# Reordering the head and the tail of a fused attention and gated-MLP kernel

## The chip, the cores and the metric

The kernel runs on one core of one Trainium2 chip. The metric is the device time in microseconds (us): the median over the runs of one kernel. Each profile shows one run, and its span is about 1.8 us shorter than the device time of that run (before: 782.7 us and 784.45 us). PE is the matmul engine (TensorE), PEld its weight load, DVE is VectorE, ACT is ScalarE, POOL is GpSimd, SP is SyncE; a q after the name means the instruction queue of that engine.

## The reference

All tensors are bf16. S is 2048, D is 512, there are 32 heads of width 16 with one shared key and value head, and F is 1792.

```python
def _A_ref(x, wq, wk, wv, wo):
    q = (x @ wq).reshape(B, S, H, Dh).transpose(0, 2, 1, 3)
    k = x @ wk
    v = x @ wv
    scores = jnp.einsum("bhqd,bkd->bhqk", q, k) * (Dh ** -0.5)
    o = jnp.einsum("bhqk,bkd->bhqd", _softmax(scores, axis=-1), v)
    return o.transpose(0, 2, 1, 3).reshape(B, S, H * Dh) @ wo

def _B_ref(x, w_gate, w_up, w_down):
    return (_silu(x @ w_gate) * (x @ w_up)) @ w_down

xn = _layernorm(x)
s = _A_ref(xn, A_wq, A_wk, A_wv, A_wo)
g = _silu(_B_ref(xn, B_w_gate, B_w_up, B_w_down))
return x + s * g
```

## The kernel before

A planner in the kernel orders all instructions when the program is built. It uses assumed durations and arrival times. `ext(t)` is an assumed arrival time, `chain` and `tadd` pin an instruction behind the one before it on the same engine. The body is a stream of 128x1024 exponentials on ACT. PE fills gaps with matmuls whose weights `zw` are zero, which is meant to keep its clock full.

The parts that the change and the argument touch (cuts are marked with `# ...`):

```python
PB_URG, AHEAD, LAZY, ACTMIN, ACTLOW = 6, 16, 8, 1.7, 1.5
# ... head: masks, loads
nc.vector.tensor_single_scalar(out=hbit[:], in_=pidx[:], scalar=DH, op=ALU.bitwise_and)
# ... two more DVE operations make hmask from hbit
nc.sync.dma_start(out=x_sb[:, 0:2, :], in_=x_v[:, 0:2, :])
nc.sync.dma_start(out=x_sb[:, 2:4, :], in_=x_v[:, 2:4, :])
# ... key, query and value weights on ACT's queue; the rest of x on SyncE
# ... blocks 2 and 3 of x: block 3's mean and variance are worked out on ACT
arr2 = ext(4.6)
a = OP("ACT", 0.65, [arr2], lambda: nc.scalar.activation(
    out=hT[:, 3, :], in_=x_sb[:, 3, :], func=ACT.Copy, accum_out=ssum[:, 0:1]), (-1,), name="asum")
# ... then a Square with accumulation; then DVE's veps of blocks 2 and 3 waits for both
# ... the planner's rule for zero matmuls: fill a gap when PE's recent activity is low
if Tz - F >= MMF + sd.switch("c") and act_ < ACTMIN:
    ...  # return F, ("zero", bb)
# ... tail
tadd("PE", tq_emit(1, [0, 1], tq01))          # transposes of the last block, f32
tadd("PE", tq_emit(1, [2, 3], tq23))
tadd("PE", e_out_mm(LN + 3, bank[st["obank"][3]][:, :D], range(NQ - 1)))   # 12 partial matmuls
# ... normalise, transpose o_tok, copy, final 8 matmuls, flag matmul
def fin_add(k, eng, nm):
    tadd(nm, e_out_add(LN + k, dsts[k], eng))
    bi = (nc.sync if k % 2 == 0 else nc.scalar).dma_start(out=out_v[:, LN + k, :], in_=res[(LN + k) % 4][:, :D])
    tadd("SP" if k % 2 == 0 else "ACT", bi)
# ... additions 0 and 2 on POOL, 1 and 3 on DVE, flag_i written between
flag = nc.values_load(flag_i[0:1, 0:1], min_val=0, max_val=1)
with tc.If(flag > 0):
    ...  # exact-maximum fallback, never taken with these inputs
```

## Time and profile before

Before the change: 785.91 us median of 3 runs (785.13 to 789.57). The profiled run had 784.45 us.

| part of the span, us | before |
|---|---|
| first statistics on x start | 3.64 |
| first statistics to first exponential | 9.83 |
| first exponential to end of the last (the body) | 755.43 |
| end of last exponential to end of DVE's last addition | 9.15 |
| from there to the end of the span (the closing) | 4.65 |
| of the body at half clock | 6.8 |

The five parts add up to the span, so a difference between two profiles can be put in one of them. The prediction below shows the lines. The timeline of the kernel before: its columns are start, duration, engine, source line, operation, tiles, and in brackets the idle time before it and what ended it.

### The profile page before, as it was taken

How to read it: one execution, taken by the hardware profiler on the slowest of the kernel's cores; microseconds unless marked ns; L12 is line 12 of the kernel's file. 1: busy time of each engine (PE TensorE's matmuls, PEld its weight loads, DVE VectorE, ACT ScalarE, POOL GpSimd, SP SyncE). 2: the span in 40 equal slices, each digit the busy share in tenths (PEclk: the TensorE clock that was granted, in tenths of full speed). 3: DMA queues.
4: the chain of work that ended last, by engine and by line, in shares of the span. 5: the costliest groups of instructions: out<-in, count | busy, mean ns of one | idle time of the engine just before them, and what ended most of it. 6: DMA issues, size and time to landing. Idle time of an engine off the chain costs nothing.

```text
span 782.7 us, 19544 instructions
## 1 busy us (share of the span) xinstructions
PE 699.4 (89%) x8149; PEld 209.0 (27%) x8150; DVE 732.4 (94%) x920; ACT 758.0 (97%) x866; POOL 50.6 (6%) x59
## 2 busy tenths in 40 slices
PE   7988888899898898999899898899988989899994
PEld 3322222222222222222222222222222222222221
DVE  7779999999999999999999999999999999999994
ACT  5999999999999999999999999999999999999993
POOL 3100000000011000000002000000001200000001
PEclk9999999999999999999999999999999999999997
DMA  9400000000011000000001000000000000000000
GB/s 328 138 9 9 15 2 23 2 10 15 3 43 35 23 1 8 18 1 16 10 23 36 22 23 2 23 3 9 17 1 23 30 22 2 1 23 2 23 2 31
DMA packets 21191, 20.07 MB, mean 26 GB/s; under 512 B 8744, under 2 KB 17192, under 8 KB 21096
## 3 DMA queue, kind: packets, MB, share of 16 engines
q1 hardware_dynamic: 19224, 17.94, 7.5%
q8 instruction: 65, 1.06, 0.6%
q10 hardware_dynamic: 1872, 0.82, 0.4%
q14 instruction: 30, 0.25, 0.1%
HBM read 14.19 MB, written 2.34 MB: 21 GB/s over the span
## 4 chain that ended last, share of the span: by engine, by line
ACT 52%; PE 26%; issue 12%; DVE 8%; DMA 1%; SPq 0%; POOL 0%; ACTq 0%; DVEq 0%
ACT Pb L934 46%; PE m_ps L485 10%; PE ring L874 10%; PE o_ps L744 5%; ACT th L654 4%; DVE Bf L988 2%; ACT th L671 1%; DVE x_sb L1007 1%; DVE Bf L1007 1%; ACT g_sb L934 1%; DMA x_sb<-in_A_x_dram 1%; DVE Bf L1014 0%; DVE Bf L1002 0%; DVE x_sb L988 0%; DVE ab L656 0%
## 5 line engine op out<-in xcount | busy, mean ns | idle before, releaser
L934 ACT ACTIVATE Pb<-ring 128x1024 bf16<-128x1024 f32 x772 | 726.0, 1133 | 3.7 <-PE ring L874 3.5
L874 PE MATMUL ring<-QB,KT 32*128 32x512 bf16 x2048 | 306.3, 384 | 60.3 <-ACT Pb L934 57.6
L988 DVE TENSOR_SCALAR Bf<-ring 128x1024 uint16<-128x1024 f32 x172 | 209.6, 1219 | 11.0 <-PE ring L874 9.2
L874 PEld LDWEIGHTS <-KT 32*128 32x128 bf16 x2048 | 92.8, 91 | 350.9 <-issue 346.9
L744 PE MATMUL o_ps<-Pb,VA 128*32 128x512 bf16 x1544 | 148.1, 385 | 0.7 <-ACT Pb L934 0.7
L1007 DVE TENSOR_TENSOR Bf<-Bf,Bf 128x2048 f16<-128x2048 f16 x74 | 90.0, 1216 | 0.1
L988 DVE TENSOR_SCALAR x_sb<-ring 128x1024 uint16<-128x1024 f32 x72 | 87.7, 1218 | 2.4 <-PE ring L874 2.2
L485 PE MATMUL m_ps<-xnT,wu_sb 128*32 128x512 bf16 x896 | 72.6, 387 | 5.2 <-DVE ab L656 5.2
L485 PE MATMUL m_ps<-wd_sb,hT 128*32 128x512 bf16 x896 | 71.5, 383 | 1.2 <-DVE g_sb L673 1.2
L485 PE MATMUL m_ps<-xnT,wg_sb 128*32 128x512 bf16 x896 | 71.5, 384 | 0.0
L744 PE MATMUL o_ps<-Bf,VD 128*32 128x512 f16 x688 | 67.9, 387 | 0.9 <-DVE Bf L1014 0.6
L729 POOL TENSOR_TENSOR oT<-oa,rb 128x512 bf16<-128x512 f32 x15 | 20.1, 1342 | 615.1 <-DMA rb<-dscr 410.5
L1014 DVE TENSOR_SCALAR Bf<-Bf 128x2048 uint16<-128x2048 uint16 x86 | 59.0, 686 | 0.5
L744 PEld LDWEIGHTS <-VA 128*32 128x32 bf16 x1560 | 38.3, 94 | 51.7 <-issue 50.1
L1002 DVE TENSOR_SCALAR Bf<-Bf 128x2048 uint16<-128x2048 uint16 x74 | 50.5, 687 | 0.0
L660 DVE TENSOR_TENSOR hT<-ab,m_ps 128x512 bf16<-128x512 f32 x56 | 38.1, 680 | 3.2 <-PE m_ps L485 3.1
L656 DVE SCALAR_TENSOR_TENSOR ab<-th,m_ps 128x512 f32<-128x512 f32 x56 | 38.1, 680 | 3.1 <-ACT th L654 3.0
L654 ACT ACTIVATE th<-m_ps 128x512 f32<-128x512 f32 x56 | 39.6, 706 | 0.0
L744 PEld LDWEIGHTS <-VD 128*32 128x32 f16 x976 | 26.2, 94 | 41.0 <-issue 37.7
L1007 DVE TENSOR_TENSOR x_sb<-x_sb 128x2048 f16<-128x2048 f16 x24 | 30.8, 1284 | 0.0
L744 PE MATMUL o_ps<-x_sb,VD 128*32 128x512 f16 x288 | 28.0, 386 | 1.1 <-DVE x_sb L1007 0.9
L485 PEld LDWEIGHTS <-wu_sb 128*32 128x32 bf16 x896 | 19.0, 95 | 34.2 <-issue 30.4
(115 smaller groups left out, 381.8 us busy)
## 6 DMA issues: line engine op xcount, KB each, us to landing
rb<-dscr SPq DMA_DIRECT2D x15, 256.0 KB
dn<-oa SPq DMA_DIRECT2D x120, 2.0 KB, 1.7
oa<-oa SPq DMA_DIRECT2D x60, 32.0 KB, 2.0
wg_sb<-in_B_w_gate_dram SPq DMA_DIRECT2D x1, 1792.0 KB, 12.5
wu_sb<-in_B_w_up_dram SPq DMA_DIRECT2D x1, 1792.0 KB
wd_sb<-in_B_w_down_dram SPq DMA_DIRECT2D x1, 1792.0 KB, 19.4
out_dram<-xn SPq DMA_DIRECT2D x14, 128.0 KB, 1.7
x_sb<-in_A_x_dram SPq DMA_DIRECT2D x3, 512.0 KB
```

The lines of the kernel that those rows point to most:

```text
L485: return [nc.tensor.matmul(out=dst[GRP * j:GRP * j + GRP, :], lhsT=w[:, GRP * j:GRP * j + GRP], rhs=rhs, start=start, stop=stop, tile_posi ...
L654: t_ = OP("ACT", 0.477, [a], lambda: nc.scalar.activation(out=th[i][:], in_=m_ps[:], func=ACT.Tanh, scale=0.5), (0,), name="tanh")
L656: s_ = OP("DVE", 0.6, [t_, ab_rel[i]], lambda: nc.vector.scalar_tensor_tensor(out=ab[i][:], in0=th[i][:], scalar=1.0, in1=m_ps[:], op0=ALU ...
L660: h = OP("DVE", 0.6, [b], lambda: nc.vector.tensor_tensor(out=hT[:, f, :], in0=ab[i][:], in1=m_ps[:], op=ALU.mult), (1,), name="hmul")
L729: return [pk, q], lambda eng: eng.tensor_tensor(out=oT[qs % 2][:, jj, :], in0=o0[:], in1=rbt[:], op=ALU.mult)
L744: r.append(nc.tensor.matmul(out=o_ps[GRP * g:GRP * g + GRP, :], lhsT=lhs, rhs=rhs, start=(n == 0), stop=(n == pv_total[(b, g)] - 1), tile_ ...
L874: return lambda: [nc.tensor.matmul(out=ring[sl][:, u * 512:(u + 1) * 512], lhsT=KT[half][GRP * g:GRP * g + GRP, t * P:(t + 1) * P], rhs=QB ...
L934: lambda: nc.scalar.activation(out=buf, in_=ring[i][:], func=ACT.Exp, scale=escale, bias=ebias),
L988: lambda: nc.vector.tensor_scalar(out=U[:, hs], in0=ring[si][:], scalar1=ubias, scalar2=UINF, op0=ALU.add, op1=ALU.min), (1.5, u), name="p ...
L1002: o1 = OP("DVE", 0.6, [pa, pa0] + wrel, lambda: nc.vector.tensor_scalar(out=Bf[wi], in0=U, scalar1=0x3FF, scalar2=0x3800, op0=ALU.bitwise_and,
L1007: return lambda: eng.tensor_tensor(out=Bf[wi][:, a:z].bitcast(FP16), in0=Bf[wi][:, a:z].bitcast(FP16), in1=U[:, a:z].bitcast(FP16), op=ALU ...
L1014: o2 = OP("DVE", 0.6, o3, lambda: nc.vector.tensor_scalar(out=U, in0=U, scalar1=0x7C00, scalar2=None, op0=ALU.bitwise_and), (2, u, 1), nam ...
```

## The change

The intent: shorten the head by loading the first rows of x ahead of the query weights and making the masks early; keep PE's clock full in the tail by issuing the partial product ahead of the transposes and adding filler matmuls; and issue all last stores from SyncE. Before the change, too, the first load of x was issued (0.72 us) ahead of that of the query weights (1.32 us). The diff, cut to its core:

```diff
-    nc.vector.tensor_single_scalar(out=hbit[:], in_=pidx[:], scalar=DH, op=ALU.bitwise_and)
+    mask_i = [None] * 3
+    mask_i[0] = nc.vector.tensor_single_scalar(out=hbit[:], in_=pidx[:], scalar=DH, op=ALU.bitwise_and)
 # ... mask_i[1], mask_i[2] likewise; the loads on ACT's queue get chain("ACT", ...),
 # ... with the warm-up activation between the key weights and the query weights
+    chain("DVE", mask_i)
-                arr2 = ext(4.6)
+                arr2 = ext(4.9)
-        if Tz - F >= MMF + sd.switch("c") and act_ < ACTMIN:
+        if Tz - F >= MMF + sd.switch("c") and (act_ < ACTMIN or cur["issued"] == NTILE):
+    tadd("PE", e_out_mm(LN + 3, bank[st["obank"][3]][:, :D], range(NQ - 1)))
     tadd("PE", tq_emit(1, [0, 1], tq01))
     tadd("PE", tq_emit(1, [2, 3], tq23))
-    tadd("PE", e_out_mm(LN + 3, bank[st["obank"][3]][:, :D], range(NQ - 1)))
+    for _ in range(2):
+        tadd("PE", nc.tensor.matmul(out=tp[0], lhsT=ident_bf[:], rhs=xnT[:, 0, 0:512], start=True, stop=True))
 # ... in fin_add
-        bi = (nc.sync if k % 2 == 0 else nc.scalar).dma_start(out=out_v[:, LN + k, :], in_=res[(LN + k) % 4][:, :D])
-        tadd("SP" if k % 2 == 0 else "ACT", bi)
+        tadd("SP", e_out_st(LN + k))
     fin_add(0, nc.gpsimd, "POOL")
     tadd("DVE", e_out_mul(LN + 1, obk[1], dsts[1]))
+    fin_add(1, nc.gpsimd, "POOL")
     tadd("DVE", e_out_mul(LN + 2, obk[2], dsts[2]))
-    fin_add(2, nc.gpsimd, "POOL")
     tadd("DVE", nc.vector.tensor_single_scalar(out=flag_i[:], in_=tq01[0:1, 0:1], scalar=P - 0.5, op=ALU.is_lt))
-    fin_add(1, nc.vector, "DVE")
     tadd("DVE", e_out_mul(LN + 3, obk[3], dsts[3]))
+    fin_add(2, nc.vector, "DVE")
     fin_add(3, nc.vector, "DVE")
```

More of the change, by code (lines that the diff above doesn't have):

```diff
@@ L323 @@
     warm = const.tile([P, 1], FP32, name="warm")
-    nc.scalar.activation(out=warm[:], in_=eps_t[:], func=ACT.Exp)
+    warm_i = nc.scalar.activation(out=warm[:], in_=eps_t[:], func=ACT.Exp)
     neg_half = const.tile([P, 8], FP32, name="neg_half")
@@ L330 @@
     hbit = const.tile([P, 1], I32, name="hbit")
-    nc.vector.tensor_single_scalar(out=hbit[:], in_=pidx[:], scalar=DH, op=ALU.bitwise_and)
+    mask_i = [None] * 3
+    mask_i[0] = nc.vector.tensor_single_scalar(out=hbit[:], in_=pidx[:], scalar=DH, op=ALU.bitwise_and)
     hmask = const.tile([P, 2], FP32, name="hmask")
-    nc.vector.tensor_scalar(out=hmask[:, 1:2], in0=hbit[:], scalar1=1.0 / DH, scalar2=None, op0=ALU.mult)
-    nc.vector.tensor_scalar(out=hmask[:, 0:1], in0=hbit[:], scalar1=-1.0 / DH, scalar2=1.0,
-                            op0=ALU.mult, op1=ALU.add)
+    mask_i[1] = nc.vector.tensor_scalar(out=hmask[:, 1:2], in0=hbit[:], scalar1=1.0 / DH, scalar2=None, op0=ALU.mult)
+    mask_i[2] = nc.vector.tensor_scalar(out=hmask[:, 0:1], in0=hbit[:], scalar1=-1.0 / DH, scalar2=1.0,
+                                        op0=ALU.mult, op1=ALU.add)
     xnT = persist.tile([P, KC, S], BF16, name="xnT")
@@ L407 @@
     with nc.allow_non_contiguous_dma(reason="tiny k/v weight loads (32B rows)"):
-        nc.scalar.dma_start(out=wk_sb[:], in_=A_wk.rearrange("(kc p) n -> p kc n", p=P))
-        nc.scalar.dma_start(out=wq_sb[:], in_=A_wq.rearrange("(kc p) n -> p kc n", p=P))
-        nc.scalar.dma_start(out=wv_sb[:], in_=A_wv.rearrange("(kc p) n -> p kc n", p=P))
+        chain("ACT", nc.scalar.dma_start(out=wk_sb[:], in_=A_wk.rearrange("(kc p) n -> p kc n", p=P)))
+        chain("ACT", warm_i)
+        chain("ACT", nc.scalar.dma_start(out=wq_sb[:], in_=A_wq.rearrange("(kc p) n -> p kc n", p=P)))
+        chain("ACT", nc.scalar.dma_start(out=wv_sb[:], in_=A_wv.rearrange("(kc p) n -> p kc n", p=P)))
     for c in range(1, NSC):
```

## The prediction

> **What bounds the kernel now.** I read the page first, then the busy time by stretches, then the timeline of the first 24 us and of the last 28 us, and last the chain of work that ended last and the branch instructions at the end. The page's busy line says which engine paces the body:
>
> ```profile
> PE 699.4 (89%) x8149; PEld 209.0 (27%) x8150; DVE 732.4 (94%) x920; ACT 758.0 (97%) x866; POOL 50.6 (6%) x59
> ```
>
> ACT is busy 97% of the span, nearly all of it in the 128x1024 exponentials (772 of them, 1133 ns each, overlapping, one every 0.90 us). Between the first exponential at 13.47 us and the last, which ends at 768.90 us, the kernel runs at ACT's pace, and the change touches nothing there. So only three things can move the time: the 13.47 us before the first exponential, the 13.8 us after the last (782.7 - 768.9), and accidents in the body. The stretches show the accidents:
>
> ```profile
> core 0: us, PE busy (x) PEld busy (x) DVE busy (x) ACT busy (x) POOL busy (x), PEclk, DMA share, GB/s
> 120.00:130.00 10.00, 8.79 (x92) 2.23 (x88) 8.78 (x11) 9.00 (x11) 0.00 (x0) 0.83 0.09 18
> ...
> 750.00:760.00 10.00, 9.69 (x98) 2.69 (x93) 9.04 (x14) 9.13 (x11) 0.00 (x0) 0.85 0.00 0
> ...
> 771.00:773.00 2.00, 1.82 (x16) 0.43 (x8) 1.76 (x10) 0.30 (x2) 0.00 (x0) 0.50 0.00 0
> ```
>
> The granted clock falls to half for 3.4 us twice in the body, and each time ACT loses about 1 us (9.00 and 9.13 busy of 10). A third drop lies in the tail, from 770.1 to 773.4 us: there PE runs at 0.50 for the whole stretch from 771 to 773. The head looks like this:
>
> ```profile
> 5.64 0.73 POOL L441 TENSOR_TENSOR rstd<-veps,neg_half 128x2 f32<-128x2 f32 x1 [0.29 <-DVE veps L438]
> ...
> 7.09 0.17 DVE L438 TENSOR_SCALAR veps<-mv 128x2 f32<-128x2 f32 x1 [0.73 <-ACT hT L530]
> ...
> 7.48 0.73 DVE L444 TENSOR_SCALAR xn<-x_sb,mv,rstd 128x512 bf16<-128x512 bf16 x2
> ...
> 8.70 0.59 ACT L455 COPY xnT<-ring 128x512 bf16<-128x512 bf16 x1 [1.55 <-PE ring L449]
> ...
> 13.47 7.44 ACT L934 ACTIVATE Pb<-ring 128x1024 bf16<-128x1024 f32 x8 [0.48 <-PE ring L874]
> ```
>
> DVE normalises the first two blocks of x (the xn line) at 7.48 us. Their scale factor (POOL's rstd) was ready at 5.64 + 0.73 = 6.37 us. The 1.1 us between is queue order: ahead of xn stands the veps of blocks 2 and 3, which waits for ACT's variance until 7.09 us, and then three mask operations that could have run in DVE's 2.4 us of idleness before x arrives at 3.64 us. The first copy of xnT and the first exponential hang on that xn. The tail:
>
> ```profile
> 769.86 1.02 PE L1042 MATMUL ring<-ident_f,oa 128*128 128x128 f32 x4 [0.52 <-DVE oa L757]
> ...
> 770.81 1.47 PE L485 MATMUL ring<-wo_sb,oT 128*32 128x512 bf16 x12
> ...
> 772.21 0.39 PE L1326 MATMUL ring<-ident_bf,o_tok 128*128 128x128 bf16 x2
> ...
> 773.94 1.29 DVE L687 SCALAR_TENSOR_TENSOR ab<-ring,g_sb 128x512 f32<-128x512 f32 x2 [0.87 <-PE ring L485]
> ...
> 775.91 1.59 POOL L692 TENSOR_TENSOR xn<-oa,x_sb 128x512 bf16<-128x512 f32 x1
> ...
> 777.12 0.93 DVE L692 TENSOR_TENSOR xn<-oa,x_sb 128x512 bf16<-128x512 f32 x1
> ```
>
> After the last block's transposes (L1042) PE runs 12 matmuls of a partial product (L485) at half clock until 772.28 us; only then come the transposes of o_tok (L1326), although their first half was written at 771.71 us. The final products end at 773.88 us, DVE multiplies from 773.94 us and ends the last addition at 778.05 us. What follows is no longer computing:
>
> ```profile
> L1359 SPq TENSOR_LOAD <-flag_i x1: 511/511/511, 776.4 to 776.4; - x1
> ...
> L1359 ACTq TENSOR_LOAD <-flag_i x1: 477/477/477, 778.5 to 778.5; - x1
> ```
> ```profile
> L1360 SPq COMPARE_BRANCH  x1: 45/45/45, 777.9 to 777.9; - x1
> L1360 ACTq COMPARE_BRANCH  x1: 54/54/54, 779.0 to 779.0; - x1
> ...
> L1360 ACTq EVENT_SEMAPHORE  x1: 17/17/17, 781.6 to 781.6; - x1
> ```
>
> ACT issues the last store at 778.08 us, loads the flag (0.48 us), compares at 779.0 us and is next seen at 781.6 us: 2.6 us for a jump. SyncE jumps at 777.9 us and is back at 780.7 us. The span ends about 1.0 us after ACT is back.
>
> **What the Trainium skill says.** "TensorE: Matmul & The Clock Gate", Part 1, has the clock fall to half after an idle window of about 3.4 us, a window that is free-running and not tied to the kernel's start. The trace agrees: 770.1 to 773.4 us is 3.3 us, and the drop near 125.0 us lies about 189 windows of 3.413 us earlier. "GPSIMD Engine Reference", 1 Specifications, has POOL share SBUF interfaces with DVE when a DVE instruction has two SBUF inputs; the trace agrees, as POOL's addition takes 1.15 us alone and 1.59 us beside DVE's additions. "Runtime: NRT & Kernel Launch", Instruction fetch mechanics, says that a taken branch outside the fetched pages stalls for a fetch; 2.6 and 2.8 us here fit it. "DMA: Bandwidth & Descriptors", Latency and other measured facts, gives a register load a floor of about 600 ns; here it took 0.48 to 0.67 us, so the measured numbers are used.
>
> **The change, part by part.** I compared the instruction order of both kernels on every engine.
>
> *Head.* On ACT nothing moves: before the change, too, the table load and the warm-up stand between the key-weight load and the query-weight load, and the x loads are untouched on SyncE. Worth 0. On DVE the masks move into the idle time, and the first two xn come ahead of the second veps, since the planner now assumes a later arrival (4.9 instead of 4.6). On POOL the building of ident_f (0.35 us) moves ahead of rstd: it starts about 5.40 us, so rstd runs from about 5.77 to 6.50 us. Then xn goes at 6.54 us instead of 7.48 us, its second one ends at 7.27 us, PE's eight transposes end at about 7.72 us and ACT copies at 7.76 us instead of 8.70 us: 0.94 us earlier. ACT is free then, its variance work ends at 7.16 us. The second scale factor, ready about 8.2 us, comes before DVE's copy ends at about 8.8 us, so it does not bind. One query-weight matmul (0.11 us apart at this size) now stands ahead of the next transposes and gives back about 0.13 us. First exponential: 13.47 - 0.94 + 0.13 = 12.66 us, a gain of 0.8 us. The query weights landed 5.8 us after issue at 1.32 us, so at about 7.1 us, before their new use at 9.3 us. The gain passes through the body whole, as no transfer is waited for there: the gate weights land 12.5 us after 3.80 us and are first used at 46.5 us.
>
> *Tail, PE.* Twenty zero matmuls (five groups of four) stand before the last accumulation. A group takes about 0.22 us at full clock: 5 x 0.22 = 1.1 us from 767.65 us, done by 768.75 us, before the last exponential releases the accumulation at 768.95 us. Cost 0. The 12 partial matmuls (3 groups, 0.65 us) now fill 769.17 to 769.82 us, while DVE copies the accumulator; the transposes start at 769.86 us as before. PE is now busy enough that I expect the clock to stay full. Then: transposes end at 770.67 instead of 770.88 us (gain 0.2); o_tok's halves are written at 771.49 and 772.13 us; its first transposes end at about 771.88 instead of 772.60 us; ACT copies at 771.92 instead of 772.70 us; the final eight matmuls start at 772.33 instead of 773.12 us and take 0.60 instead of 0.76 us. DVE's multiplications start at about 772.98 instead of 773.94 us: gain 0.95 us.
>
> *Tail, DVE, POOL, SyncE.* DVE has the same four multiplications, flag and two additions, with one wait less, and ends at about 776.95 instead of 778.05 us. That would be 1.1 us. But the queue behind it changes. POOL has additions 0 and 1 back to back: 773.82 to 774.97, then to between 776.1 us (alone) and 776.5 us (slowed by DVE's additions). SyncE, in order, issues store 1 after that (0.35), loads the flag (0.51, with some 0.1 for two small instructions), issues stores 2 and 3 (0.35 each) and compares: 1.75 us with gaps, so at 776.3 + 1.75 = 778.05 us. It is back 2.8 us later at 780.85 us, checks eight DMA semaphores in 0.6 us (as from 780.7 to 781.3 us before), and the closing barrier takes 0.9 us: 782.35 us against 782.7 us. Of the 1.1 us won on DVE only 0.35 us reaches the end.
>
> Sum: 0.8 + 0.35 = 1.15 us.
>
> **Rivals.** (a) *The stores do not bind:* POOL is quick and SyncE's flag load hides. Then the compare goes 0.4 us after DVE's last addition, at 777.4 us, and the tail is worth up to 1.0 us, the change 1.8 us, time 783.8. For it: SyncE waited for POOL only shortly before. Against it: the flag load stands between stores 1 and 2. (b) *The fillers hurt or the clock still drops:* at half clock the zeros take 5 x 0.43 = 2.15 us, end at 769.8 us, and push the last accumulation back by 0.85 us; the tail then loses about 0.5 us and the change is worth 0.3 us, time 785.2. For it: the window's phase is free. Against it: PE was dense from 760 to 767 us. (c) *The body swamps it:* one clock drop more or less is 1 us, as large as the gain, and its place depends on the phase at launch. The runs before spread from 785.13 to 789.57 us. (d) *The head gain is eaten* if POOL's second scale factor or the query weights come late: then 0.35 us remains, time 785.2.
>
> **The range and the chances.** As base I take 785.5, midway between the two closer runs (785.13 and 785.91), since 789.57 is an outlier. 785.5 - 1.15 = 784.35, rounded to 784.4 us. The mechanisms allow 783.7 to 785.3; drops of the clock widen it by about 1 us, more upward as the runs before do: 783.0 to 786.3. Two per cent is 15.7 us, more than the whole head or the whole tail, so faster by that is 0.01, slower 0.01, the same 0.98.
>
> **What would show it.** Right: the masks before the first statistics, xn at about 6.5 us, first exponential at 12.5 to 12.8 us; query weights issued at about 1.3 us as before; granted clock 1.00 from 770 to 773 us; the first o_tok transposes by 771.6 us; DVE's last addition ending near 777 us; SyncE, not ACT, last at the branch. Wrong: a first exponential at 13.4 us (the head chain is elsewhere), a clock of 0.50 after 770 us (the fillers miss), an interval between first and last exponential that differs by over 1 us (the body decided), or a time above 786.3 us.

## More of the kernel before

```profile
5.25 0.63 ACT L525 ACTIVATE hT<-x_sb 128x512 bf16<-128x512 bf16 x1 [2.50 <-DMA x_sb<-in_A_x_dram]
```

ACT's variance of block 3 of x starts when that block has landed, at 5.25 us, which is 1.61 us after DVE started on the first blocks.

## The result

After: 786.21 us median of 6 runs (785.83 to 788.06). Before, 6 runs (the 3 known ones included): 786.40 us (785.13 to 789.57). The ratio is 0.9994, with a 95% interval of 0.997 to 1.0018: the same. A ratio here is always the mean time of one kernel's runs over that of the other's of the same rounds, so it is not quite the ratio of the medians quoted.

The profiled run of after was its slowest (788.06 us). Its parts beside those of before:

| part of the span, us | before | after | difference |
|---|---|---|---|
| first statistics on x start | 3.64 | 3.99 | +0.35 |
| first statistics to first exponential | 9.83 | 8.93 | -0.90 |
| body | 755.43 | 758.33 | +2.90 |
| last exponential to DVE's last addition | 9.15 | 8.40 | -0.75 |
| closing | 4.65 | 6.65 | +2.00 |
| span | 782.7 | 786.3 | +3.6 |
| of the body at half clock | 6.8 | 17.1 | +10.3 |

The page of after, the busy line and the granted clock in 40 slices:

```profile
PE 703.2 (89%) x8172; PEld 209.3 (27%) x8172; DVE 731.8 (93%) x920; ACT 758.2 (96%) x866; POOL 49.9 (6%) x59
...
PEclk9989999999999999999999999999999999999987
```

PE got 23 matmuls more in the records; the other engines are where they were. Next, the same stretches as in the prediction, in the view of busy time by stretches (columns: stretch, length, busy time and instruction count of each engine, granted clock, DMA share, GB/s), with one early stretch added:

```profile
47.00:62.00 15.00, 13.89 (x130) 3.27 (x129) 11.88 (x15) 13.19 (x16) 0.00 (x0) 0.77 0.01 2
120.00:130.00 10.00, 8.38 (x102) 2.44 (x94) 9.98 (x14) 10.00 (x13) 0.00 (x0) 1.00 0.08 16
...
750.00:760.00 10.00, 9.35 (x74) 2.27 (x73) 7.69 (x11) 7.95 (x9) 0.00 (x0) 0.66 0.00 0
771.00:773.00 2.00, 2.00 (x29) 0.91 (x19) 0.76 (x2) 0.26 (x1) 0.00 (x0) 1.00 0.00 0
```

From 120 to 130 us the clock is now full and ACT is busy for 10.00 of 10 us. From 750 to 760 us it is at 0.66 instead of 0.85, and from 47 to 62 us at 0.77. In the tail, from 771 to 773 us, it is 1.00 where before had 0.50. The head of after, from the timeline:

```profile
6.05 0.73 POOL L444 TENSOR_TENSOR rstd<-veps,neg_half 128x2 f32<-128x2 f32 x1
...
6.81 0.74 DVE L447 TENSOR_SCALAR xn<-x_sb,mv,rstd 128x512 bf16<-128x512 bf16 x2
...
7.46 0.17 DVE L441 TENSOR_SCALAR veps<-mv 128x2 f32<-128x2 f32 x1
...
8.04 0.58 ACT L458 COPY xnT<-ring 128x512 bf16<-128x512 bf16 x1 [1.28 <-PE ring L452]
...
12.92 7.44 ACT L937 ACTIVATE Pb<-ring 128x1024 bf16<-128x1024 f32 x8 [0.48 <-PE ring L877]
```

Now xn stands ahead of the veps of blocks 2 and 3, and the first exponential comes at 12.92 us although x came 0.35 us later. The tail:

```profile
770.02 1.25 PE L747 MATMUL o_ps<-xnT,zw 128*32 128x512 bf16 x20
...
771.32 1.03 PE L488 MATMUL ring<-wo_sb,oT 128*32 128x512 bf16 x12
...
772.28 0.71 PE L1045 MATMUL ring<-ident_f,oa 128*128 128x128 f32 x4
...
775.40 1.29 DVE L690 SCALAR_TENSOR_TENSOR ab<-ring,g_sb 128x512 f32<-128x512 f32 x2 [0.21 <-PE ring L488]
...
776.23 2.26 POOL L695 TENSOR_TENSOR xn<-ab,x_sb 128x512 bf16<-128x512 f32 x2 [37.26 <-DVE ab L690]
...
777.87 1.78 DVE L695 TENSOR_TENSOR xn<-oa,x_sb 128x512 bf16<-128x512 f32 x2
```

The last exponential ends at 771.25 us. DVE multiplies 775.40 - 771.25 = 4.15 us later, where before took 773.94 - 768.90 = 5.04 us. But the last addition (the DVE L695 group of two) ends at 779.65 us, 8.40 us after the exponential, so a part of the gain is gone by then. The view of the flag's tile shows who loads it when (durations in ns, then the start in us):

```profile
L1363 ACTq TENSOR_LOAD <-flag_i x1: 462/462/462, 777.4 to 777.4; - x1
...
L1363 SPq TENSOR_LOAD <-flag_i x1: 513/513/513, 778.9 to 778.9; - x1
```

The view of the line of the branch, in after:

```profile
L1364 SPq EVENT_SEMAPHORE  x8: 17/17/17, 784.3 to 784.9; - x8
L1364 ACTq COMPARE_BRANCH  x1: 50/50/50, 777.9 to 777.9; - x1
...
L1364 DVEq COMPARE_BRANCH  x1: 72/72/72, 778.7 to 778.7; - x1
L1364 ACTq EVENT_SEMAPHORE  x1: 17/17/17, 780.6 to 780.6; - x1
...
L1364 SPq COMPARE_BRANCH  x1: 50/50/50, 781.9 to 781.9; - x1
```

ACT loads the flag early now, at 777.4 us, jumps at 777.9 us and is back at 780.6 us. SyncE is the last one to the branch, at 781.87 us, 2.2 us after DVE's last addition; before, it was there 0.1 us ahead of the end of it. One reason is the third store (of four), in the view of the output tensor, cut to a stretch that holds only this store:

```profile
L698 SPq DMA_DIRECT2D out_dram<-xn x1: 1143/1143/1143, 779.9 to 779.9; - x1
```

Its issue alone takes 1.143 us, where the other three take 0.34 to 0.37 us.

### The profile page after: what moved, and what is told of

Read it like the earlier page. It is cut to its first block, busy times and chain, and to the rows that moved or that the text cites. A ratio compares the mean times of both kernels' runs of the same rounds, so it can differ in the third digit from the quotient of the medians.

```text
span 786.3 us, 19589 instructions
## 1 busy us (share of the span) xinstructions
PE 703.2 (89%) x8172; PEld 209.3 (27%) x8172; DVE 731.8 (93%) x920; ACT 758.2 (96%) x866; POOL 49.9 (6%) x59
## 3 DMA queue, kind: packets, MB, share of 16 engines
q8 instruction: 66, 1.08, 0.6%
## 4 chain that ended last, share of the span: by engine, by line
ACT 52%; PE 28%; issue 12%; DVE 7%; POOL 1%; SPq 0%; DMA 0%; ACTq 0%; DVEq 0%; POOLq 0%
ACT Pb L937 45%; PE ring L877 11%; PE m_ps L488 10%; PE o_ps L747 5%; ACT th L657 4%; DVE Bf L991 1%; ACT th L674 1%; DVE Bf L1010 1%; ACT g_sb L937 1%; DVE x_sb L991 1%; DVE ab L659 0%; DVE Bf L1017 0%; DVE Bf L1005 0%; DVE g_sb L676 0%; DVE xnT L458 0%
```

## The experiments

Twelve kernels ran, all with correct results. All the timed runs were fast; runs of "one look" are single runs, whose state is unknown, and from them I read only the parts of the span. Those parts (us; in e9_flag_late DVE's end is that of the flag, 0.06 us after the last addition):

| run | to first exponential | body | body at half clock | last exp. to DVE's end | closing |
|---|---|---|---|---|---|
| before | 9.83 | 755.43 | 6.8 | 9.15 | 4.65 |
| after | 8.93 | 758.33 | 17.1 | 8.40 | 6.65 |
| e1_stores_back | 8.92 | 755.41 | 6.8 | 8.25 | 4.88 |
| e2_stores_only | 9.91 | 759.10 | 17.1 | 9.38 | 6.72 |
| e3_head_only | 8.94 | 757.52 | 13.6 | 9.15 | 4.85 |
| e4_no_fill | 8.93 | 760.86 | 23.9 | 8.39 | 6.13 |
| e5_flag_last | 8.91 | 756.15 | 10.3 | 8.39 | 6.84 |
| e6_two_queues | 8.91 | 759.32 | 17.1 | 8.39 | 4.86 |
| e7_fill23 | 8.94 | 753.84 | 0.0 | 8.24 | 4.75 |
| e8_fill26 | 8.93 | 756.24 | 3.4 | 8.26 | 4.85 |
| e9_flag_late | 8.92 | 761.84 | 27.3 | 8.45 | 6.00 |
| e10_before_fill | 9.24 | 754.06 | 0.0 | 8.25 | 4.92 |
| e11_after_fill | 8.96 | 754.54 | 0.0 | 8.39 | 6.17 |
| e12_best | 8.97 | 753.87 | 0.0 | 8.23 | 4.44 |

My first theory was that the change gains 0.9 us in the head and 0.75 us on PE and DVE in the tail, that the closing takes it back, and that the clock in the body adds noise larger than either. The rival was that the body itself had become slower through the change.

### e1_stores_back: after, with the additions and stores of before

```diff
-        tadd("SP", e_out_st(LN + k))
+        bi = (nc.sync if k % 2 == 0 else nc.scalar).dma_start(out=out_v[:, LN + k, :], in_=res[(LN + k) % 4][:, :D])
+        tadd("SP" if k % 2 == 0 else "ACT", bi)
 # ... and additions 0 and 2 on POOL, 1 and 3 on DVE, in the order of before
```

> The changed kernel with only the last additions and stores put back as before (additions 0 and 2 on POOL, stores alternating between SyncE and ACT). Theory A (the all-SyncE stores with the flag load between them cost the tail what its PE part wins): from the end of DVE's last addition to the end of the span about 4.7 us as before, not 6.65; DVE's last addition still ends 8.2 to 8.5 us after the last exponential (9.15 before); time about 1.5 us under the changed kernel. Rival B (the longer close is an accident of that one trace, of fetching at the jump): the close stays near 6.6 us or the changed kernel's other executions do not have it, and the time does not move.

Measured: 784.62 us median of 6 runs (783.11 to 791.21), before 787.13 us of 11 runs in the same rounds (784.16 to 791.85); ratio 0.999, interval 0.9955 to 1.0025, the same. The closing falls back to 4.88 us, and DVE ends 8.25 us after the last exponential. The body is 755.41 us, as in before with the same time at half clock, so the body did not become slower through the change. The spread of 8 us within one kernel hides the timed difference; the parts of the span do not suffer from it.

### e2_stores_only: before, with the additions and stores of after

```diff
-        tadd("SP" if k % 2 == 0 else "ACT", bi)
+        tadd("SP", e_out_st(LN + k))
 # ... and additions 0 and 1 on POOL, 2 and 3 on DVE
```

> The kernel before with only the last additions and stores as in the changed one. Theory A: SyncE is last at the branch, one store issue is long (over 1 us), the close grows from 4.65 to over 6 us, time 1.5 to 2 us over before. Rival B: close 4.6 to 5.0 us, time as before within 0.5 us.

Measured: 789.53 us median of 6 (786.47 to 792.29), ratio 1.0027, interval 0.9996 to 1.0059: not clearly apart. The closing is 6.72 us, as in after. The third store's issue took 1.129 us, the fourth's 0.554 us. So the closing of after belongs to the stores and the additions and to nothing else in the change.

### e3_head_only: before, with the early masks and the later assumed arrival

```diff
+    mask_i = [None] * 3   # ... the three mask operations collected, as in the change
+    chain("DVE", mask_i)
-                arr2 = ext(4.6)
+                arr2 = ext(4.9)
```

> The kernel before with only the early masks, the later assumed arrival (4.9) and the ACT order. Theory: first exponential 0.8 us earlier than before once the arrival of x is taken out (statistics of the first block to first exponential 9.8 us before, 8.9 us in the changed kernel); last exponential to the end of the span 13.8 us as before; the time moves by whatever the clock drops of the body do, plus or minus 3 us. Rival (the early rstd order on POOL does it, not DVE): cannot be told here.

Measured, one look: 785.99 us; 8.94 us from the statistics to the first exponential. These two edits make the whole head; which of them does how much was not separated. The order of the loads on ACT, which the expectation names but the edit leaves out, has no part in it.

### e4_no_fill: after, without the 20 zero matmuls and the 2 fillers of the tail

```diff
-        if Tz - F >= MMF + sd.switch("c") and (act_ < ACTMIN or cur["issued"] == NTILE):
+        if Tz - F >= MMF + sd.switch("c") and act_ < ACTMIN:
-    for _ in range(2):
-        tadd("PE", nc.tensor.matmul(out=tp[0], lhsT=ident_bf[:], rhs=xnT[:, 0, 0:512], start=True, stop=True))
```

> The changed kernel without the twenty zero matmuls and the two filler matmuls. Theory C (fillers keep the clock up): a window of half clock falls into the 5 us after the last exponential, as in the kernel before, and the last exponential to the end of DVE's last addition takes 8.8 us or more instead of 8.39. Rival D (moving the partial product alone does it): clock 1.00 through the final products and 8.3 to 8.5 us.

Measured, one look: 790.12 us, with 23.9 us of the body at half clock. In the tail the clock stayed full all the same, and DVE ended 8.39 us after the last exponential, as in after. Busy time by stretches, in the three us after the last exponential at 773.68 us:

```profile
773.70:774.70 1.00, 0.96 (x14) 0.35 (x13) 0.53 (x2) 0.00 (x0) 0.00 (x0) 1.00 0.00 0
774.70:775.70 1.00, 0.71 (x6) 0.40 (x4) 0.39 (x2) 0.00 (x0) 0.00 (x0) 1.00 0.00 0
775.70:776.70 1.00, 0.28 (x2) 0.11 (x2) 0.88 (x5) 0.02 (x1) 0.00 (x0) 1.00 0.00 0
```

The 12 partial matmuls alone, now ahead of the transposes, fill the first of these stretches to 0.96. The fillers were not needed in this run.

### e5_flag_last: after, with SyncE's flag load behind its four stores

```diff
+    for bi in flag_loads:
+        if "SP" in str(bi.ins.engine):
+            tc.add_manual_dep(bi.ins, _last["SP"].ins.name, _nosync, reason="order")
```

> The changed kernel with SyncE's flag load forced behind its four stores. It splits the 2.0 us by which the close grew. Theory A1 (the flag load between the second and third store delays both later stores): the third store is issued right after DVE's addition and takes 0.35 us, the compare comes about 1.3 us after DVE's end, close 5.6 to 5.9 us. Theory A2 (SyncE issues slowly because the other engines fetch at their jumps just then): the third store is still over 0.8 us long and the close stays at 6.2 us or more.

Measured, one look: 785.93 us; the closing is 6.84 us, no shorter. All four stores, in the view of the output tensor (durations in ns: least, median, most):

```profile
L698 SPq DMA_DIRECT2D out_dram<-xn x4: 344/344/999, 775.1 to 777.4; - x4
```

The long one, 0.999 us, is now the fourth store, which starts at 777.4 us; the third, from 776.8 us, took 0.344 us, as A1 had it. But a store is still long, and the closing is no shorter. So SyncE's own flag load, which had stood just ahead of the long store in after, is not what lengthens it.

### e6_two_queues: after, with stores 0 and 1 on SyncE, 2 and 3 on ACT, ACT's flag load ahead of its stores

```diff
-        tadd("SP", e_out_st(LN + k))
+        bi = (nc.sync if k < 2 else nc.scalar).dma_start(out=out_v[:, LN + k, :], in_=res[(LN + k) % 4][:, :D])
+        tadd("SP" if k < 2 else "ACT", bi)
 # ... the flag loads of ACT and SyncE chained behind the writing of flag_i
```

> The changed kernel with stores 0 and 1 on SyncE and 2 and 3 on ACT, both queues loading the flag before DVE's last additions. If the close is set by when SyncE reaches its compare (compare to end 4.8 us in the kernel before, 4.4 in the changed one), SyncE compares about 1 us before DVE's end and the close falls under 4.65 us, to 4.1 to 4.4 us, set by ACT's jump or the last store's landing. If instead the last store's landing sets it whatever the queue, the close is 4.6 to 5.0 us as before.

Measured, one look: 787.27 us; the closing is 4.86 us, as with the alternating stores. ACT's two stores:

```profile
L1349 ACTq DMA_DIRECT2D out_dram<-xn x2: 370/756/1143, 780.0 to 780.6; - x2
```

The second one, from 780.6 us, took 1.143 us. So the long issue is not peculiar to SyncE's queue. The additions are here those of after, and the closing is short all the same: by this run, what lengthens it is that all four stores are on one queue.

### e9_flag_late: after, with the flag written behind the last addition

```diff
-    tadd("DVE", nc.vector.tensor_single_scalar(out=flag_i[:], in_=tq01[0:1, 0:1], scalar=P - 0.5, op=ALU.is_lt))
     tadd("DVE", e_out_mul(LN + 3, obk[3], dsts[3]))
     fin_add(2, nc.vector, "DVE")
     fin_add(3, nc.vector, "DVE")
+    tadd("DVE", nc.vector.tensor_single_scalar(out=flag_i[:], in_=tq01[0:1, 0:1], scalar=P - 0.5, op=ALU.is_lt))
```

> The kernel after, with the flag computed only after the last addition, so that every engine's flag load and jump comes after VectorE's additions; all four stores on SyncE. Theory A2 (the third store's issue is stretched by what the other engines do at their flag loads and jumps): no engine jumps while the stores are issued, so the third store takes about 0.35 us, as the others do. Rival: the third store still takes 0.8 us or more, so that the other engines' jumps are not the cause. The stretch from the end of VectorE's additions to the end of the span: about 5.5 to 6.0 us by A2, 6.6 or more by the rival (after: 6.65).

Measured, one look: 790.78 us, with 27.3 us of the body at half clock; the closing is 6.00 us. The last three stores, in the view of the output tensor:

```profile
L698 SPq DMA_DIRECT2D out_dram<-xn x3: 332/333/343, 781.8 to 783.0; - x3
```

And the view of the line of the branch:

```profile
L1364 SPq EVENT_SEMAPHORE  x8: 17/17/17, 787.1 to 787.6; - x8
L1364 ACTq COMPARE_BRANCH  x1: 50/50/50, 783.7 to 783.7; - x1
...
L1364 SPq COMPARE_BRANCH  x1: 50/50/50, 784.6 to 784.6; - x1
```

With no engine at its branch before 783.7 us, no store took more than 0.343 us. The rival (0.8 us or more whatever the other engines do) has fallen. Put beside the other runs: every long issue (after 1.143, e2 1.129, e4 0.789, e5 0.999, e6 1.143, e11 0.632, e12 0.736 us) began 1.6 to 2.4 us after the first engines' compare, with at least PE, POOL and DVE already past theirs. Yet e4's third store, 2.0 us after the first compare, took 0.34 us, and ACT's last store in e10_before_fill, 1.6 us after it and 0.2 us after DVE's, took 0.36 us. So the jumps go with the long issues, but neither their number nor the delay tells when one comes.

The traces also hold the transfers that bring instructions, and these tell more. In after one of 16 KB runs on DMA queue q8 from 779.10 to 780.66 us; the third store's issue runs from 779.88 to 781.02 us. The view of the DMA queues of after from 779.0 to 779.2 us holds the start of this one packet (packets, MB, share of 16 engines):

```profile
q8 instruction: 1, 0.02, 48.7%
```

In all 14 traces such a transfer starts 0.95 to 1.6 us after PE's compare. All seven long issues began while one was under way and ended 0.26 to 0.45 us after it had ended. In e9_flag_late none ran while the last stores were issued. And the branch is not needed for it: in the bodies of the 14 traces (from 30 us on), where no engine is at a branch, 120 issues of SyncE took over 0.25 us more than is usual for their tensor, up to 1.88 us in all. Every one of them overlaps such a transfer and ends 0.29 to 0.39 us after it; of the other issues in the bodies about 6% overlap one. So a long issue is one that waits for an instruction transfer to end, as far as this coincidence shows; the jumps matter here by the transfer that follows them. It is not the whole condition: ACT's last store in before ran inside such a transfer and took 0.36 us. Which engine's instructions q8 brings, and why some issues escape, stays open.

### e7_fill23 and e8_fill26: e1_stores_back, with more zero matmuls in the body

```diff
-PB_URG, AHEAD, LAZY, ACTMIN, ACTLOW = 6, 16, 8, 1.7, 1.5
+PB_URG, AHEAD, LAZY, ACTMIN, ACTLOW = 6, 16, 8, 2.3, 1.5     # e8_fill26: 2.6
```

> The kernel of the run with the stores put back, and the planner's activity limit for zero matmuls raised from 1.7 to 2.3 (828 instead of 176 zero matmuls). Theory E (the body's time is 753.3 us plus 1.08 us for each window of 3.41 us at half clock, as the six traces so far give): fewer half-clock windows, none to two, first to last exponential 753 to 755.5 us, time about 781 to 783 us, and a narrower spread than 783.1 to 791.2. Rival F (the zeros get in the way of the scores on PE): the clock stays up but the body takes 756 us or more.

> The same with the limit at 2.6 (1092 zero matmuls). Theory E: no half-clock window in the body, 753 to 754 us there, 780 to 782 us in all with a spread under 2 us. Rival F: a longer body than with 2.3 at the same clock.

Measured: e7_fill23, with 828 instead of some 176 zero matmuls, 781.76 us median of 6 (781.45 to 782.06); before 786.98 us of 12 runs in the same rounds; ratio 0.9935, interval 0.9912 to 0.9959. e8_fill26, with 1092, 783.93 us of 6 (782.60 to 786.08); ratio 0.9964, interval 0.9938 to 0.9990. The spread of e7_fill23 is 0.6 us where before has 7.7 us in the same rounds. The page of e7_fill23, busy line and granted clock:

```profile
PE 736.7 (94%) x8822; PEld 224.0 (29%) x8824; DVE 731.5 (94%) x920; ACT 756.9 (97%) x866; POOL 51.9 (7%) x59
...
PEclk9999999999999999999999999999999999999998
```

The clock is full in all slices but the last, and ACT is busy for 10.00 of 10 us from 120 to 130 us and from 750 to 760 us, where before lost 1.00 and 0.87 us. The noise of the body is the clock: before's own runs in these rounds go from 784.16 us at a mean granted clock of 0.990 to 791.85 us at 0.976. The body column of the table above gives its price: from before to e4_no_fill the body grows by 760.86 - 755.43 = 5.43 us for (23.9 - 6.8) / 3.41 = 5.0 windows more at half clock, 1.08 us for each. e3_head_only and e9_flag_late lie within 0.1 us of that line, the others with the old threshold within 0.7 us. The kernels with 828 zeros lie 0.6 to 1.3 us above it. e8_fill26 has one such window (3.4 us) and is 1.9 us above the line, 753.3 + 1.08, so rival F came true there. That more zeros than needed stand in the way of work fits this, but it rests on one trace.

When does a window fall? I cut the trace of before into windows of 3.413 us that start where a half-clock stretch starts. The view by stretches, same columns as above, with PE's busy time as first entry after the length:

```profile
114.76:118.17 3.41, 2.72 (x36) 0.89 (x36) 3.38 (x5) 3.41 (x5) 0.00 (x0) 1.00 0.00 0
...
121.59:125.00 3.41, 2.20 (x27) 0.69 (x30) 3.39 (x5) 3.41 (x6) 0.00 (x0) 0.99 0.18 37
125.00:128.40 3.40, 3.40 (x28) 0.64 (x24) 2.63 (x4) 2.40 (x4) 0.00 (x0) 0.51 0.04 10
...
746.20:749.60 3.40, 2.16 (x24) 0.64 (x16) 3.40 (x5) 3.40 (x5) 0.00 (x0) 1.00 0.00 0
...
766.70:770.10 3.40, 1.75 (x12) 0.59 (x11) 0.72 (x2) 2.19 (x3) 0.00 (x0) 0.99 0.00 0
770.10:773.50 3.40, 3.10 (x24) 1.00 (x26) 1.89 (x11) 0.65 (x2) 0.00 (x0) 0.51 0.00 0
```

The windows ahead of the three drops have PE busy for 2.20, 2.16 and 1.75 of 3.41 us, shares of 0.65, 0.64 and 0.52; a share of 0.80 (114.76 us) is followed by a full clock. Cut in this way, the bodies of all 14 traces give: each of the 10 windows at full clock with a share of 0.635 to 0.644 was followed by half clock; of 26 windows from 0.645 to 0.69, 16 were; of some 3000 above 0.69, three were, with shares of 0.73 (after, at 746.5 us) and 0.89 (e4_no_fill and e9_flag_late, at 24 us). So a low share stands ahead of 26 of the 29 drops; what caused the other three is open. Outside the bodies, four windows with a share of 0.57 to 0.63 were not followed by a drop: in the heads of before and e2, in the tails of e4_no_fill and e12_best. The body of before has stretches near that edge, and which of them coincides with a window depends on the phase at launch: hence the spread, as far as the traces show. In e7_fill23 I slid a window over the body in steps of 0.34 us: the least share at any phase was 0.72, against 0.64 in before. In e8_fill26 one stretch at 678 us still had 0.65, and the one half-clock window follows it.

### e10_before_fill, e11_after_fill, e12_best: the parts with the clock held full

e10 and e11 are before and after with `ACTMIN` at 2.3 as above. e12_best is e7_fill23 with three of the stores on ACT:

```diff
-        bi = (nc.sync if k % 2 == 0 else nc.scalar).dma_start(out=out_v[:, LN + k, :], in_=res[(LN + k) % 4][:, :D])
+        bi = (nc.sync if k == 0 else nc.scalar).dma_start(out=out_v[:, LN + k, :], in_=res[(LN + k) % 4][:, :D])
 # ... and ACT's flag load chained ahead of its second store
```

> The kernel before with the filler threshold of the whole body raised (828 zero matmuls instead of some 176), as in e7_fill23. If that keeps the clock full, the noise of the body is gone and the time should be that of e7_fill23 plus what the head and the TensorE tail of the change are worth: 781.76 + 0.9 (head) + 0.75 to 0.9 (tail) = 783.3 to 783.6 us, with a spread of the runs below 1.5 us. Rival (the parts are worth nothing once the clock is full, since ScalarE's body takes up the lead): 781.8 us.

> The kernel after with the same raised threshold. If the closing part (all stores on SyncE) costs 1.9 to 2.0 us beside e7_fill23, which differs from it in nothing else: 783.7 us. Together with e10_before_fill this shows whether the parts cancel: the two should differ by 0.5 us or less (-0.9 head, -0.75 tail, +2.0 closing). Rival (the closing costs 0.75 us, as predicted): 782.5 us, a full 0.9 us below e10_before_fill.

> e7_fill23 with the first store on SyncE, the other three on ScalarE, and ScalarE's flag load between its first and second, to let SyncE, the engine whose jump ends last, go to its flag earlier. If SyncE's jump and checks set the end: the stretch from VectorE's last addition to the end of the span falls from 4.75 to 4.1 to 4.4 us, and the time to 781.2 to 781.5 us. If the landing of the last store or ScalarE's own jump sets it: 781.8 us or a little more, as e7_fill23.

Measured, in rounds on one chip with before at 785.65 us of 11 runs (782.14 to 788.29):

| kernel | median, us | range of 6 runs | ratio to before, 95% interval |
|---|---|---|---|
| e10_before_fill | 782.36 | 781.88 to 784.26 | 0.9962 (0.9936 to 0.9989) |
| e11_after_fill | 783.61 | 782.51 to 783.99 | 0.9967 (0.9941 to 0.9993) |
| e12_best | 781.70 | 781.07 to 782.25 | 0.9947 (0.9922 to 0.9973) |

e11_after_fill came as expected by itself, but not within 0.5 us of e10_before_fill, as that did not come as expected: I had expected 783.3 to 783.6 us, from a gain of 0.9 us in the head and 0.75 to 0.9 us in the tail that it should lack. Its profile shows that it lacks neither in full, and that corrected my theory in two places.

First, the tail. From the timeline of e10_before_fill, whose last exponential ends at 767.13 us:

```profile
768.09 0.77 PE L1042 MATMUL ring<-ident_f,oa 128*128 128x128 f32 x4 [0.52 <-DVE oa L757]
...
769.75 0.29 PE L1326 MATMUL ring<-ident_bf,o_tok 128*128 128x128 bf16 x2
...
771.27 1.29 DVE L687 SCALAR_TENSOR_TENSOR ab<-ring,g_sb 128x512 f32<-128x512 f32 x2 [0.22 <-PE ring L485]
```

The order on PE is that of before, with the transposes first. Yet DVE multiplies 4.14 us after the last exponential (before: 5.04, after: 4.15) and ends at 8.25 us (before: 9.15, e7_fill23 with the new order: 8.24). All that the new order gains in the tail is the clock. Before, PE's share in the window ahead was 0.52 and the next ran at half clock; in after the corresponding window has 0.87, in e4_no_fill 0.73. Where the clock is full anyway, the order is worth nothing.

Second, the head. ACT's variance chain starts with the landing of block 3 of x. The timeline of ACT in e10_before_fill, which has the head of before:

```profile
4.86 0.63 ACT L525 ACTIVATE hT<-x_sb 128x512 bf16<-128x512 bf16 x1 [2.11 <-DMA x_sb<-in_A_x_dram]
...
13.07 7.44 ACT L934 ACTIVATE Pb<-ring 128x1024 bf16<-128x1024 f32 x8 [0.48 <-PE ring L874]
```

And in e2_stores_only, which has it too:

```profile
5.69 0.63 ACT L525 ACTIVATE hT<-x_sb 128x512 bf16<-128x512 bf16 x1 [2.95 <-DMA x_sb<-in_A_x_dram]
...
13.90 7.44 ACT L934 ACTIVATE Pb<-ring 128x1024 bf16<-128x1024 f32 x8 [0.48 <-PE ring L874]
```

From that start to the first exponential it is 8.21 us in both, and 13.47 - 5.25 = 8.22 us in before. With the new head the first exponential comes 8.91 to 8.97 us after the first statistics, in all eleven traces, whatever block 3 does. So the gain is the lag of block 3 behind the first blocks, less 8.93 - 8.21 = 0.72 us: 1.61 - 0.72 = 0.89 us in before, 0.98 in e2, 0.31 in e10 (lag 1.03 us). In the traces with the new head the lag was 0.83 to 1.65 us, in five of eleven under 0.9 us, so an estimate of the usual gain from these is 0.1 to 0.6 us, with 0.9 at the upper end. Below a lag of 1.03 us no trace of the old head shows the gain. Why the lag varies is open.

With the clock full, the profiles of e11 and e10 differ by -0.28 us (head), +0.14 us (DVE's end), +1.25 us (closing) and +0.48 us (body). The medians differ by +1.25 us; the means by 0.57 us, as two runs of e10 stand at 784.08 and 784.26 us with a slightly lower clock (0.994 and 0.995 against 0.996 and above). I call this slower by about 1 us, not settled to better than half of that.

e12_best closes in 4.44 us instead of the 4.75 us of e7_fill23, just above the 4.1 to 4.4 us expected, and is 0.06 us away in the median, on another chip: no timed gain is shown. Its third store on ACT took 0.736 us, so this order has a long issue too. The expectation took SyncE for the engine whose jump ends last; in e7_fill23 ACT was back later (778.57 us, SyncE 777.83 us).

Both kernels beat before in their rounds: e7_fill23 by 0.65%, e12_best by 0.53%, clear of zero but far below 2%. After was not run in these rounds; its median was 786.21 us.

## Why the prediction was right or wrong

The prediction of the same (within 2%) was right, and the time of 786.21 us lies in the range of 783.0 to 786.3 us, at its upper edge. Neither says much about the mechanism: 2% is 15.7 us, and that the time stayed inside the range by 0.1 us is luck, as two errors pushed it up. It is 1.8 us above the 784.4 us predicted. Of that, 0.9 us is the base: 785.5 us was taken, midway between two of three runs, and six runs have a median of 786.40 us; the third run, set aside as an outlier, was none (the runs of before in the whole study reach from 782.14 to 791.85 us). The other 0.96 us is the change: 1.15 us expected, 0.19 us found.

- *Head.* "a gain of 0.8 us": right for the profiled run. The step from first statistics to first exponential fell by 0.90 us, and the order, with xn ahead of the second veps and the query weights issued as before, is as described. What was taken as a constant is the wait for ACT's variance; it is the landing of block 3, which differs from run to run, and the gain with it (0.31 us in e10_before_fill). With the lag of after's own profile, 0.87 us, the old head would have lost only 0.87 - 0.72 = 0.15 us. That 0.8 us came out is the luck of a late block in the profile of before.
- *Tail, PE.* "DVE's multiplications start at about 772.98 instead of 773.94 us: gain 0.95 us": found 5.04 - 4.15 = 0.89 us, and the clock stayed full as expected. The reason given mixed the order with the clock. e10_before_fill shows that the clock is all of it.
- *Tail, DVE.* "That would be 1.1 us": found 0.75 us. Addition 2, now on DVE, runs beside POOL's second addition: it started at 777.87 us and took 1.18 us, against 0.67 us for an addition of DVE in before. The prediction had the slowing fall on POOL; POOL's second addition took 1.15 us, as alone. With the additions of before (e1_stores_back) the end came at 8.25 us.
- *Tail, SyncE.* This is the step that failed: "1.75 us with gaps" from the end of POOL's second addition to SyncE's compare. It took 781.87 - 778.49 = 3.38 us. The order of the queue was right, its terms were too small: the third store took 1.14 instead of 0.35 us, two register instructions with their gaps between flag load and store took 0.46 instead of 0.1 us, and 0.37 us pass between the last store and the compare. The long store runs beside the instruction transfer described under e9_flag_late, which the prediction did not have. So the tail as a whole, from the last exponential to the end, is 15.05 us in after against 13.80 us in before: a loss of 1.25 us, not a gain of 0.35 us.
- *Rivals.* (a) fell: SyncE's stores do bind. (b) fell: the fillers were harmless, and the clock did not drop. (c), the body swamps it, is what the timed runs show: 10.3 us more at half clock go with a profiled body 2.9 us longer. A body that differs by over 1 us was one of the prediction's own signs of being wrong. (d) holds in a milder form, by the landing of block 3 and not by POOL or the query weights.

So the gain was given back in the closing. Head and tail gained 0.9 + 0.75 us in the profiles, the closing took 2.0 us. With a usual head gain of some 0.4 us the change costs slightly under 1 us; with the full one, 0.35 us. Both are below what six runs with such a spread can tell from zero, and the timed medians, 0.19 us apart the other way, do not contradict it.

## What to carry to other kernels

Before the ends of a kernel are tuned, make the body quiet: a higher threshold for filler matmuls, which raised the least share of PE in any stretch of 3.4 us from 0.64 to 0.72, was worth more (3.3 us in the medians of e10_before_fill, with nothing else changed) than all the reordering, and narrowed the spread from 6.2 to 2.4 us in the same rounds. Read a gain by its cause: an order that helps only because the clock drops, or only because one block lands late, is worth little in the run where that does not happen. At the end of a program, count every instruction of the last queue up to its branch, and do not put all last stores on one queue.

## What the Trainium skill lacked or had wrong

- "TensorE: Matmul & The Clock Gate", Part 1, has the clock fall after an idle window, and says of another kernel that micro-idles between groups of matmuls make it oscillate; it gives no share. The window ahead of a drop was not idle here: PE was busy for 0.64 and 0.65 of it in the body of before. Of the 29 drops in the bodies, 26 followed a share of 0.64 to 0.69, three one of 0.73 or 0.89. The length and the free-running phase agree (189 windows of 3.413 us between two drops).
- No page found gives the price of a half-clock window where another engine sets the pace: 1.08 us for each 3.41 us, in this body paced by ACT.
- "DMA: Bandwidth & Descriptors", Rules for kernel authors, says that spreading DMAs over several engines only saves the sequencers' issue time. That agrees, but at the end of a program this is time on the path: with all four stores on SyncE the closing took 6.0 to 6.8 us, with two queues 4.4 to 4.9 us.
- No page found says that the issue of a DMA can wait for a transfer of instructions: instead of 0.33 to 0.37 us, seven of the last stores took 0.63 to 1.14 us, each ending 0.26 to 0.45 us after such a transfer, and 120 issues in the bodies did the like.
- No page found gives the time from a compare at the end of a program, with a branch that is not entered, to the end: from SyncE's compare it was 4.3 to 5.2 us in every trace.
